# Linear attention, then a gated mixture of causal-attention experts: the work as a task graph, PE's order from a list scheduler

## The chip, the cores and the metric

One core of a Trainium2 chip runs the whole program. The engines are TensorE (PE, with its weight loads as PEld), VectorE (DVE), ScalarE (ACT), GpSimd (POOL) and SyncE (SP, which issues the DMAs here). The time is device microseconds of one execution; several executions are run, and one more is profiled.

## The reference

Eight batches, eight heads of 64, 576 tokens. The first half is linear attention without a softmax, normalised for each head; the second half gives each token its two best of four experts, each of which is a causal attention over the batch's tokens.

```python
kv = einsum('bhsd,bhse->bhde', k, v)
out = einsum('bhsd,bhde->bhse', q, kv)
x = out / sqrt(mean(out * out, -1) + 1e-6) * g_norm      # heads side by side: (8, 576, 512)
logits = x @ w_gate                                      # 4 experts; softmax over the best 2
for e in range(4):
    q, k, v = x @ wq[e], x @ wk[e], x @ wv[e]            # 64 wide
    a = softmax(causal(q @ k.T / 8))
    result += gate[e] * (a @ v @ wo[e])
```

## The kernel before

Each batch goes through three stages. The 576 tokens are five blocks (four of 128, one of 64); heads and experts are taken in pairs. PSUM is cut into three "big" buffers of two banks and two "small" ones of one bank, and every product on PE takes one of them.

Stage A (stage_a): p_kv is k by v for each head, over the tokens; it is copied to kvx (DVE) and, padded to two heads side by side, to kv2 (ACT). kv2 is transposed on PE (p_kt, L216), copied to kvT, and multiplied by the gate weights (p_kg, L224, four products), so that four more columns per head in kvx give the gate's logits. q is transposed block by block (p_q, L200, copied to qT by DVE). Then p_out (L242) is q by kvx for each block; DVE copies it to the one o_sb (L249), ACT squares it out of p_out (L253), DVE sums the squares (L259). A row of small DVE instructions makes the inverse root (L270 to L280) and the logits (L285, L291), and POOL scales o_sb to x_tok (L297).

Stage X (stage_x): x_tok is transposed on PE (p_x, L313) and copied by ACT to xT.

Stage S (stage_s): DVE makes the gate; p_v (L355), then for each pair of experts the projections p_proj (L373), copied by ACT to qTp and kT (L384, one copy for both experts, 64 partitions each). The scores p_sc (L400) contract over the 64 partitions of one expert; five pieces a pair; ACT takes their exp to PT (L410), POOL masks the diagonal blocks (L415). p_O (L451) is PT by v with a column of ones; DVE divides and gates it (L467 to L472) to osc, which is transposed (p_OT, L484). The stage final gives p_y (L506), copied by ACT and stored by SP.

The order: every stage is a Python generator that yields after each step the PE time that its writer gives it. merge takes from three streams at a time, by these times: stage S of batch b (whose own steps follow a string of letters), stage X of batch b + 1 and stage A of batch b + 2. This gives the program order; the framework then sets the order of every engine's instructions, PE's too, from that program order and from what it finds ready by its own timing. Loads of batch b + 3 are issued at the start of turn b. The three projection weights are loaded to one staging buffer, one after the other (L158), and scaled by g_norm on DVE (L159).

Of the kernel before, what the change touches and what calls it, by code (L numbers as in the profile page):

```python
# [14 lines left out]
AX_X = mybir.AxisListType.X  # L15


@with_exitstack
def kernel(
# [45 lines left out]
    def small(shape, name, dtype=FP32):
        return ps1.tile(shape, dtype, tag="small", name=name)
# [6 lines left out]
    kr, vr, kvx, kv2s, sqs, lg8s, kTs, vexts, mss = [], [], [], [], [], [], [], [], []  # L73
    for j in range(2):
# [16 lines left out]
        nc.gpsimd.memset(t[:], 1.0)  # L91
        vexts.append(t)
        t = const.tile([P, NB, H], FP32, name=f"ms{j}")
        nc.gpsimd.memset(t[REM:P, NF], 1.0)
        mss.append(t)
    ob = const.tile([P, NB, H, GW], FP32, name="o_sb")
    nc.gpsimd.memset(ob[REM:P, NF], 0.0)
    for j in range(3):
        t = const.tile([P, H, Dh + 1], FP32, name=f"sq{j}")
        nc.gpsimd.memset(t[:, :, Dh : Dh + 1], 1e-6)  # L100
        sqs.append(t)
    zpad = const.tile([P, NB * P - S], FP32, name="zpad")
    nc.gpsimd.memset(zpad[:], 0.0)
    for j in range(3):
        t = const.tile([P, NB * P], FP32R, name=f"kT{j}")
        nc.vector.tensor_copy(out=t[:, S : NB * P], in_=zpad[:])
        kTs.append(t)


    def load_qkv(b, fine=False):  # L110
        qt = qkvp.tile([P, NB, H, Dh], FP32, tag="q_b", name="q_b")
        kt = qkvp.tile([P, H, NF, Dh], FP32, tag="k_b", name="k_b")
        vt = qkvp.tile([P, H, NF, Dh], FP32, tag="v_b", name="v_b")

        def main(dst, src, h0, h1):
            nc.sync.dma_start(
                dst[:, h0:h1, :, :].rearrange("p h j d -> p h (j d)"),
                src[b, h0:h1, 0 : NF * P, :].rearrange("h (p j) d -> p h (j d)", j=NF),
            )

        def rem(dst, src):
            nc.sync.dma_start(
                dst[0:REM, :, :], src[b, :, NF * P : S, :].rearrange("h p d -> p h d")
            )

        step = 2 if fine else H
# [12 lines left out]
    loads = {0: load_qkv(0, fine=True)}

    g_wide = const.tile([P, 1], FP32, name="g_wide")
    for r in range(P // Dh):
        nc.sync.dma_start(g_wide[r * Dh : (r + 1) * Dh, :], g_norm.unsqueeze(1))
    wg_st = const.tile([P, NCH, E], FP32, name="wg_st")
    nc.sync.dma_start(wg_st[:], moe_w_gate.rearrange("(c p) e -> p c e", p=P))
    wg_bd = const.tile([P, NCH, 2, E], FP32, name="wg_bd")
    nc.gpsimd.memset(wg_bd[:], 0.0)
    for hh in range(2):
        pp = slice(hh * Dh, (hh + 1) * Dh)
        nc.vector.tensor_scalar_mul(  # L150
            out=wg_bd[pp, :, hh, :], in0=wg_st[pp], scalar1=g_wide[pp]
        )
    w_r = {}
    for name, wdram in (("v", moe_wv), ("q", moe_wq), ("k", moe_wk)):
        wr = const.tile([P, NCH, E, Hd], FP32R, name=f"w{name}_r")
        wf = wst.tile([P, NCH, E, Hd], FP32, name="w_stage", tag="w_stage")
        for e in range(E):
            nc.sync.dma_start(wf[:, :, e, :], wdram[e].rearrange("(c p) f -> p c f", p=P))  # L158
        nc.vector.tensor_scalar_mul(  # L159
            out=wr[:].rearrange("p c e f -> p (c e f)"),  # L160
            in0=wf[:].rearrange("p c e f -> p (c e f)"),
            scalar1=g_wide[:],
        )
        w_r[name] = wr
    loads[1] = load_qkv(1)
    wo_st = wst.tile([P, EP, D], FP32, name="wo_st", tag="w_stage")
    for pr in range(EP):
        nc.sync.dma_start(
            wo_st[:, pr, :], moe_wo[2 * pr : 2 * pr + 2].rearrange("two d m -> (two d) m")
        )  # L170
    wo_b = const.tile([P, EP, D], BF16, name="wo_b")
    nc.vector.tensor_copy(out=wo_b[:], in_=wo_st[:])

    def kv_pair(p_kv, c, kb, vb, krem, vrem):
        for j in range(NF + 1):
            for hh in range(2):
                h = 2 * c + hh
                lk, rv = (kb[:, h, j, :], vb[:, h, j, :]) if j < NF else (krem[:, h, :], vrem[:, h, :])
                nc.tensor.matmul(  # L179
                    p_kv[hh * Dh : (hh + 1) * Dh, c, :], lhsT=lk, rhs=rv,  # L180
                    start=(j == 0), stop=(j == NF), skip_group_check=True,
                )

    def kv_copy(p_kv, kvb, kv2):
        for hh in range(2):
            pp = slice(hh * Dh, (hh + 1) * Dh)
            nc.vector.tensor_copy(out=kvb[pp, :, hh, 0:Dh], in_=p_kv[pp, :, :])
            nc.scalar.copy(kv2[pp, :, hh * Dh : (hh + 1) * Dh], p_kv[pp, :, :])  # L188


    def stage_a(b, res):
        qb, kb, vb = loads[b]
        qT = s1.tile([P, NCH, S], FP32, tag="qT", name="qT", bufs=1)
        kvb, kv2 = kvx[b % 2], kv2s[b % 2]

        def q_block(i):
            t0, nt = blocks[i]
            p_q = small([P, NCH, P], "p_q")
            for c in range(NCH):
# [341 lines left out]
    for _ in y_gen:  # L541
        pass
# [30 lines left out]
```

## Time and profile before

| | us |
|---|---|
| median of three runs | 328.1 (328.66, 324.1, 328.1) |
| the profiled execution | 324.47 |
| its span, first to last instruction | 322.5 |
| PE busy (share of the span) | 276.0 (86%) |
| PEld, weight loads | 220.4 (68%) |
| DVE | 189.2 (59%) |
| ACT | 153.0 (47%) |
| POOL | 79.5 (25%) |
| mean granted clock of TensorE | 0.945 |

An engine's busy time is the time in which at least one of its instructions runs; the end of a matmul is modelled, so that neighbours overlap in it. A clock of 1.00 is 2.4 GHz, 0.50 is 1.2 GHz.

### The profile page before, as it was taken

The numbers are of one execution on the slowest core, as the hardware profiler recorded it, in microseconds if no ns is written. First come the engines' busy times: TensorE is split into PE (matmuls) and PEld (weight loads), VectorE is DVE, ScalarE is ACT, GpSimd is POOL, SyncE is SP. The second block draws the span as 40 slices with busy tenths as digits, with TensorE's granted clock in tenths as the row PEclk, the third lists the DMA queues.
The fourth block names the chain that finished last, engine by engine and source line by source line (L and its number), as shares of the span: only waits on it lengthen the run. The fifth ranks groups of instructions, "written<-read, shape, count | busy, mean of one in ns | idle before, by whom it ended". The sixth has DMA issues, their size and how long they took to land.

```text
span 322.5 us, 6704 instructions
## 1 busy us (share of the span) xinstructions
PE 276.0 (86%) x2624; PEld 220.4 (68%) x2624; DVE 189.2 (59%) x537; ACT 153.0 (47%) x273; POOL 79.5 (25%) x148
## 2 busy tenths in 40 slices
PE   1675579799979997999889996999889996999984
PEld 1565468588858775887667875887667875867641
DVE  0249948846884568646775578546774578424130
ACT  0203123653464654545554554545555554585843
POOL 8100600441044110702053101612052101630210
PEclk9959599999999999799999999799999999899977
DMA  6977999999704269194608372001200120021124
GB/s 195 243 199 195 205 301 223 298 180 276 152 2 133 64 202 192 41 253 127 169 3 269 81 182 58 2 0 67 82 2 2 65 83 0 0 100 53 65 83 147
DMA packets 75280, 40.30 MB, mean 125 GB/s; under 512 B 54000, under 2 KB 70384, under 8 KB 75248
## 3 DMA queue, kind: packets, MB, share of 16 engines
q1 hardware_dynamic: 75248, 39.86, 47.1%
q8 instruction: 21, 0.34, 0.5%
q14 instruction: 11, 0.09, 0.1%
HBM read 30.42 MB, written 9.44 MB: 124 GB/s over the span
## 4 chain that ended last, share of the span: by engine, by line
PE 70%; DVE 10%; ACT 9%; SPq 4%; issue 3%; POOL 1%; DMA 1%; DVEq 0%; ACTq 0%; POOLq 0%
PE p_proj L373 11%; PE p_out L242 11%; PE p_v L355 7%; PE p_sc L400 7%; PE p_O L451 7%; PE p_y L506 6%; PE p_q L200 6%; PE p_x L313 6%; PE p_kv L179 5%; ACT PT L410 3%; PE p_kg L224 3%; DVE o_sb L249 3%; SPq L134 2%; PE p_OT L484 2%; POOL x_tok L297 1%
## 5 line engine op out<-in xcount | busy, mean ns | idle before, releaser
L415 POOL TENSOR_SCALAR_AFFINE_SELECT PT<-PT 128x256 bf16<-128x256 bf16 (+1 forms) x80 | 29.3, 381 | 143.4 <-ACT PT L410 143.4
L410 ACT ACTIVATE PT<-p_sc 128x576 bf16<-128x576 f32 (+3 forms) x80 | 53.9, 714 | 20.1 <-PE p_sc L400 18.1
L297 POOL TENSOR_TENSOR x_tok<-o_sb,y 128x512 f32<-128x512 f32 (+1 forms) x40 | 42.0, 1080 | 85.1 <-DVE y L280 85.0
L242 PE MATMUL p_out<-kvx,qT 128*128 128x136 f32 (+1 forms) x320 | 48.1, 292 | 0.0
L400 PE MATMUL p_sc<-qTp,kT 64*128 64x288 f32 (+2 forms) x192 | 35.7, 358 | 10.7 <-ACT PT L410 5.9
L242 PEld LDWEIGHTS p_out<-kvx,qT 128*128 128x128 f32 (+1 forms) x320 | 40.2, 181 | 4.8 <-ACT sq L253 2.1
L253 ACT ACTIVATE sq<-p_out 128x512 f32<-128x512 f32 (+1 forms) x40 | 23.8, 596 | 39.9 <-DVE o_sb L249 38.4
L318 ACT CAST xT<-p_x 128x512 fp32r<-128x512 f32 (+1 forms) x40 | 21.8, 545 | 34.3 <-PE p_x L313 34.3
L400 PEld LDWEIGHTS p_sc<-qTp,kT 64*128 64x128 f32 x192 | 19.8, 185 | 21.9 <-ACT PT L410 8.5
L179 PE MATMUL p_kv<-v_b,k_b 128*64 128x64 f32 x512 | 25.7, 260 | 10.3 <-DMA v_b<-in_v_dram 10.3
L249 DVE COPY o_sb<-p_out 128x544 f32<-128x544 f32 (+1 forms) x40 | 28.7, 719 | 7.7 <-PE p_out L242 7.2
L362 DVE CAST vext<-p_v 128x256 bf16<-128x256 f32 (+1 forms) x40 | 17.0, 425 | 26.3 <-PE p_v L355 25.6
L259 DVE TENSOR_REDUCE ms<-sq 128x8 f32<-128x520 f32 (+1 forms) x40 | 27.4, 688 | 7.9 <-ACT sq L253 7.8
L205 DVE COPY qT<-p_q 128x512 f32<-128x512 f32 (+1 forms) x40 | 24.7, 634 | 11.6 <-PE p_q L200 11.0
L451 PEld LDWEIGHTS <-PT 128*128 128x128 bf16 (+2 forms) x480 | 24.1, 103 | 10.8 <-issue 5.3
L179 PEld LDWEIGHTS p_kv<-v_b,k_b 128*64 128x64 f32 x512 | 23.0, 173 | 12.2 <-DMA k_b<-in_k_dram 6.7
L451 PE MATMUL p_O<-vext,PT 128*128 128x65 bf16 (+2 forms) x480 | 30.3, 199 | 0.4 <-ACT PT L410 0.4
L313 PE MATMUL p_x<-ident_f,x_tok 128*128 128x128 f32 (+1 forms) x160 | 25.9, 289 | 5.4 <-POOL x_tok L297 4.3
L355 PE MATMUL p_v<-wv_r,xT 128*128 128x256 f32 (+1 forms) x160 | 28.3, 300 | 0.7 <-ACT kv L188 0.7
L373 PE MATMUL p_proj<-xT,wk_r 128*128 128x288 f32 x128 | 24.3, 314 | 3.6 <-ACT qTp L384 3.6
L506 PE MATMUL p_y<-wo_b,OT 128*128 128x512 bf16 (+1 forms) x80 | 25.1, 417 | 0.7 <-ACT OT L489 0.7
L511 ACT COPY y<-p_y 128x512 f32<-128x512 f32 (+1 forms) x40 | 23.0, 595 | 5.0 <-PE p_y L506 2.7
(67 smaller groups left out, 360.9 us busy)
## 6 DMA issues: line engine op xcount, KB each, us to landing
q_b<-in_q_dram SPq DMA_DIRECT2D x32, 256.0 KB, 5.2
out_dram<-y SPq DMA_DIRECT2D x32, 256.0 KB, 2.1
k_b<-in_k_dram SPq DMA_DIRECT2D x7, 1024.0 KB, 6.0
v_b<-in_v_dram SPq DMA_DIRECT2D x7, 1024.0 KB, 10.2
k_b<-in_k_dram SPq DMA_DIRECT2D x4, 256.0 KB, 4.7
v_b<-in_v_dram SPq DMA_DIRECT2D x4, 256.0 KB, 4.9
k_rem<-in_k_dram SPq DMA_DIRECT2D x8, 128.0 KB, 9.2
v_rem<-in_v_dram SPq DMA_DIRECT2D x8, 128.0 KB, 7.5
```

The costliest lines, as they stand in the source:

```text
L179: nc.tensor.matmul(p_kv[hh * Dh : (hh + 1) * Dh, c, :], lhsT=lk, rhs=rv, start=(j == 0), stop=(j == NF), skip_group_check=True,)
L242: nc.tensor.matmul(p_o[:nt, c // 2, (c % 2) * 2 * GW : (c % 2 + 1) * 2 * GW], lhsT=qT[:, c, t0 : t0 + nt], rhs=kvb[:, c, :, :].rearrange(" ...
L249: nc.vector.tensor_copy(out=ob[:nt, i].rearrange("p (k h) g -> p k (h g)", k=2), in_=p_o[:nt, :, 0 : 4 * GW])
L297: nc.gpsimd.tensor_tensor(out=xt[:nt], in0=ob[:nt, i, :, 0:Dh], in1=y[:nt, i * H : (i + 1) * H].unsqueeze(2).to_broadcast([nt, H, Dh]), op ...
L313: nc.tensor.transpose(p_x[:, c, :nt], xts[i][:nt, 2 * c : 2 * c + 2, :].rearrange("p h d -> p (h d)"), ident_f[:nt, :nt],)
L355: nc.tensor.matmul(p_v[:nt, :], lhsT=xT[:, c, t0 : t0 + nt], rhs=w_r["v"][:, c, :, :].rearrange("p e f -> p (e f)"), start=(c == 0), stop= ...
L373: nc.tensor.matmul(p_p[:, s, 0:HALF], lhsT=w_r[nm][:, c, 2 * pr : 2 * pr + 2, :].rearrange("p e f -> p (e f)"), rhs=xT[:, c, s * HALF : (s ...
L400: nc.tensor.matmul(p_s[:, el, o : o + hi - lo], lhsT=kTp[pb, kb * P : (kb + 1) * P], rhs=qTp[pb, lo:hi], start=True, stop=True,)
L410: nc.scalar.activation(PT[:, :, d0 : d0 + o], p_s[:, :, 0:o], ACTF.Exp, scale=scale)
L415: nc.gpsimd.affine_select(out=d, in_=d, compare_op=AluOpType.is_ge, fill=0.0, base=0, pattern=[[0, 2], [1, w]], channel_multiplier=-1,)
L451: nc.tensor.matmul(p_O[:nq, bank, (2 * n + el) * (Hd + 1) : (2 * n + el + 1) * (Hd + 1)], lhsT=PT[:nk, el, col : col + nq], rhs=vx[:nk, kb ...
L506: nc.tensor.matmul(p_y[:nq, :], lhsT=OT[:, pr, s0 : s0 + nq], rhs=wo_b[:, pr, :], start=(pr == 0), stop=(pr == EP - 1),)
```

## The change

The program is written again as tasks. graph names each task with its engine, a time for which it holds the engine, a time to its result, the tasks that it needs and the buffers that it uses. plan goes through them as a list scheduler: at each step it takes the task that can start first on any engine, and among those of that engine that can start within 0.02 of it the one with the least urgency value; a buffer is taken with the first task that uses it and given back after the last. Urgency is the batch's number times PERIOD plus an offset for each kind of task, with steps within a kind. The tasks are written out in the order of their planned start. Under manual_schedule PE keeps just that order. The instructions of DVE, ACT, POOL and SP are written in the same order too, but the framework orders them as it did before.

Some of the work changes its form. k and v of batches after the first are loaded in two pieces. The projection weights are loaded in halves to six buffers, which are those of x_tok. The p_kv copy of ACT is one copy without padding, p_kt has two transposes of two head pairs packed together in place of four, p_kg two products in place of four, and its copy to kvx is two. ACT's square reads o_sb. kT is now four buffers, one for each of the four experts, with the 64 partitions of the other expert of the pair zero; ACT copies each half by itself, and the scores contract over 128 partitions. The other tasks do what the functions of before do. The middle of the diff, with the parts that are only moved left out:

```diff
+def graph(B):
+    t = {}
+
+    def add(name, eng, hold, lat, needs=(), tiles=()):
+        t[name] = (eng, hold, lat, [n for n in needs if n in t], list(tiles))
+
+    def pe(name, hold, needs, tiles=()):
+        add(name, "PE", hold, hold + 0.27, needs, tiles)
...
+    R5, R4, R2 = range(NB), range(NCH), range(EP)
+    for b in range(B):
+        for p in R4 if b == 0 else R2:
+            w = 1.0 if b == 0 else 2.0
+            tl = (("k", b), ("v", b))
+            add(("lk", b, p), "SP", 0.5, 0.45 * w, [("kv", b - 2, c) for c in R4] if p == 0 else [], tl[:1])
+            add(("lv", b, p), "SP", 0.5, 0.45 * w, [("kv", b - 2, c) for c in R4] if p == 0 else [], tl[1:])
...
+            for nm in "qkv":
+                for p in R2:
+                    add(("lw", nm, p), "SP", 1.0, 1.3, (), (("x", nm, p),))
+                    dve(("ws", nm, p), 0.48, [("lw", nm, p), ("lg0",)], (("x", nm, p),))
...
+        for c in R4:
+            piece = c if b == 0 else c // 2
+            pe(("kv", b, c), 0.88, [("lk", b, piece), ("lv", b, piece), ("lr", b)], (("sm", "kv", b), ("k", b), ("v", b)))
+        dve(("kvx", b), 0.84, [("kv", b, c) for c in R4] + [("out", b - 2, i) for i in R5], (("sm", "kv", b),))
+        act(("kvc", b), 0.37, [("kvx", b), ("kt", b - 2)], (("sm", "kv", b),))
...
+        pe(("kt", b), 0.22, [("kvc", b)], (("sm", "kt", b),))
+        dve(("ktc", b), 0.42, [("kt", b)], (("sm", "kt", b), ("kvT", b)))
+        pe(("kg", b), 0.45, [("ktc", b), ("wg",)], (("sm", "kg", b), ("kvT", b)))
+        dve(("kgc", b), 0.34, [("kg", b)] + [("out", b - 2, i) for i in R5], (("sm", "kg", b),))
+        for i in R5:
+            pe(("out", b, i), 0.93, [("qc", b, i), ("kvx", b), ("kgc", b)], (("bg", "out", b, i), ("qT", b)))
+            dve(
+                ("oc", b, i), 0.73, [("out", b, i), ("xm", b - 1, i), ("gl", b - 1), ("sq", b - 1, i)],
+                (("bg", "out", b, i),),
+            )
+            n = NB * b + i - 3
+            act(("sq", b, i), 0.60, [("oc", b, i), ("red", n // NB, n % NB)])
+            dve(("red", b, i), 0.69, [("sq", b, i), ("nw", b - 2, 10)])
...
+        for p in R2:
+            for nm in "qk":
+                pe((nm + "p", b, p), 1.06, xT + [("ws", nm, 0), ("ws", nm, 1)], (("bg", nm, b, p), ("xT", b)))
+            act(("qpc", b, p), 0.64, [("qp", b, p)], (("bg", "q", b, p), ("qTp", b, p)))
+            act(("kpc", b, p), 1.24, [("kp", b, p)] + [("sc", b - 1, p, j) for j in R5], (("bg", "k", b, p),))
+            hold = (0.25, 0.25, 0.39, 0.28, 0.29)
+            took = (0.66, 0.66, 0.95, 0.72, 0.60)
+            for j in R5:
+                pe(("sc", b, p, j), hold[j], [("qpc", b, p), ("kpc", b, p)], (("bg", "sc", b, p, j), ("qTp", b, p)))
+                act(("exp", b, p, j), took[j], [("sc", b, p, j)], (("bg", "sc", b, p, j), ("PT", b, p)))
+                if j != 1:
+                    pool(("msk", b, p, j), 0.41 if j < 4 else 0.70, [("exp", b, p, j)])
...
+        for i in R5:
+            pe(("y", b, i), 0.45, [("otc", b, 0), ("otc", b, 1), ("wo", "o", 0), ("wo", "o", 1)], (("sm", "y", b, i), ("OT", b)))
+            act(("yc", b, i), 0.59, [("y", b, i)], (("sm", "y", b, i), ("y", b, i)))
+            add(("st", b, i), "SP", 0.1, 0.9, [("yc", b, i)], (("y", b, i),))
+    return t
+
+
+NF = 4
+POOLS = {
+    "k": 2, "v": 2, "q": 2, "sm": 2, "bg": 3, "qT": 1, "kvT": 2, "gl": 2, "x": 6, "xT": 2, "gate": 2,
+    "qTp": 3, "PT": 3, "osc": 2, "inv": 2, "OT": 2, "y": 4,
+}
+PERIOD = 25.7
+OFFSET = dict(
+    lk=-101.2, lv=-101.2, lr=-101.2, lq=-86.0, lg0=-200, wg=-60, lw=-35.8, ws=-10.8, lwo=-85, wo=-30,
+    kv=-61.6, kvx=-60.6, kvc=-60.6, q=-57.9, qc=-75.4, kt=-138.5, ktc=-138.5, kg=-137.5, kgc=-137.5,
+    out=-27.6, oc=112.9, sq=29.9, red=-136.3, nw=93.2, gl=94.2, lg=95.2, xm=24.8, x=-29.3, xc=-80.7,
+    m8=19.2, sh=19.2, ex=19.2, mk=19.2, gt=19.2, den=19.2, rd=19.2, gate=19.2, v=2.0, vc=-91.6, qp=40.7,
+    qpc=12.5, kp=35.4, kpc=7.2, sc=-1.2, exp=-49.5, msk=4.3, pv=-109.0, rc=-99.4, iv=-99.4, oc2=-99.4,
+    ot=13.9, otc=13.9, y=26.5, yc=-17.4, st=26.5,
+)
+STEP = dict(
+    x=1.5, xc=2.0, out=1.9, oc=1.9, sq=1.9, red=1.9, v=0.9, vc=0.5, y=1.7, yc=2.0, st=1.6, lq=1.5,
+)
+SECOND = 9.2
+
+def urgency(n):
+    kind = n[0]
+    if len(n) == 1 or isinstance(n[1], str):
+        return OFFSET[kind] + ("qkvo".index(n[1]) if len(n) > 1 else 0.0)
+    o = n[1] * PERIOD + OFFSET[kind]
+    if kind in STEP:
+        o += n[2] * STEP[kind]
+    elif kind in ("qp", "qpc", "kp", "kpc", "sc", "exp", "msk", "pv", "rc", "iv", "oc2", "ot", "otc"):
+        o += n[2] * SECOND + (0.4 * n[3] if len(n) > 3 else 0.0)
+    elif kind == "kv":
+        o += 0.1 * n[2]
+    return o
+
+def plan(tasks, pools, prio):
+    slots = {p: [0.0] * n for p, n in pools.items()}
+    users, need, waits = {}, {}, {}
+    for n, (_, _, _, needs, tiles) in tasks.items():
+        for tl in tiles:
+            users[tl] = users.get(tl, 0) + 1
+        need[n] = len(needs)
+        for m in needs:
+            waits.setdefault(m, []).append(n)
+    cand = {e: set() for e in ("PE", "ACT", "DVE", "POOL", "SP")}
+    for n in tasks:
+        if not need[n]:
+            cand[tasks[n][0]].add(n)
+    free = {e: 0.0 for e in cand}
+    ready, held, last, dma, order, end = {n: 0.0 for n in tasks}, set(), {}, 0.0, [], 0.0
+    none = 1e9
+    while len(order) < len(tasks):
+        starts = []
+        for eng, ns in cand.items():
+            f = free[eng]
+            for n in ns:
+                t = ready[n]
+                for tl in tasks[n][4]:
+                    if tl not in held:
+                        t = max(t, min(slots[tl[0]], default=none))
+                if eng == "PE" and t > f - 0.15:
+                    t += 0.1
+                starts.append((max(t, f), prio[n], eng, n))
+        t0, _, eng, _ = min(starts)
+        t, _, _, n = min(((t, p, e, n) for t, p, e, n in starts if e == eng and t <= t0 + 0.02), key=lambda x: x[1])
+        assert t < none
+        _, hold, lat, _, tiles = tasks[n]
+        cand[eng].discard(n)
+        for tl in tiles:
+            if tl not in held:
+                held.add(tl)
+                slots[tl[0]].remove(min(slots[tl[0]]))
+        free[eng] = t + hold
+        fin = t + lat
+        if eng == "SP":
+            dma = max(dma, t + hold + 1.3) + lat
+            fin = dma + 0.5
+        end = max(end, fin)
+        order.append((t, len(order), n))
+        for tl in tiles:
+            users[tl] -= 1
+            last[tl] = max(last.get(tl, 0.0), fin)
+            if not users[tl]:
+                slots[tl[0]].append(last[tl])
+        for m in waits.get(n, ()):
+            need[m] -= 1
+            ready[m] = max(ready[m], fin)
+            if not need[m]:
+                cand[tasks[m][0]].add(m)
+    order.sort()
+    return order, end
...
+    kTs = []
+    for pr in range(EP):
+        pair = []
+        for el in range(2):
+            t = const.tile([P, NB, P], FP32R, name=f"kT{pr}{el}")
+            other = slice((1 - el) * Hd, (2 - el) * Hd)
+            nc.vector.tensor_copy(
+                out=t[other], in_=zrow[other].unsqueeze(1).to_broadcast([Hd, NB, P])
+            )
+            nc.vector.tensor_copy(out=t[:, NF, REM:P], in_=zrow[:, REM:P])
+            pair.append(t[:].rearrange("p n t -> p (n t)"))
+        kTs.append(pair)
...
+    def lw(nm, m):
+        wf = buf(("x", nm, m), [P, 2, E, Hd], FP32, "w_stage")
+        for c in range(2):
+            rows = slice((2 * m + c) * P, (2 * m + c + 1) * P)
+            nc.sync.dma_start(wf[:, c, :, :], w_dram[nm][:, rows, :].rearrange("e p f -> p e f"))
...
+    def kvc_copy(b):
+        nc.scalar.copy(kvcs[b % 2][:], small(None, "kv", b)[:])
...
+    def kt(b):
+        p_kt = small([P, EP, P], "kt", b)
+        for m in range(EP):
+            nc.tensor.transpose(
+                p_kt[:, m, :], kvcs[b % 2][:, 2 * m : 2 * m + 2, :].rearrange("p c e -> p (c e)"), ident_f[:]
+            )
...
+    def kg(b):
+        p_kg = small([P, EP, 2, 2, E], "kg", b)
+        for m in range(EP):
+            nc.tensor.matmul(
+                p_kg[:, m].rearrange("p c a e -> p (c a e)"),
+                lhsT=tiles["kvT", b][:, m, :],
+                rhs=wg_bd[:, m].rearrange("p c a e -> p (c a e)"),
+                start=True,
+                stop=True,
+            )
...
+    def sq_act(b, i):
+        nt = blocks[i][1]
+        nc.scalar.activation(
+            sqs[(NB * b + i) % 3][:nt, :, 0:Dh], ob[:nt, i, :, 0:Dh], ACTF.Square, scale=1.0 / (Dh**0.5)
+        )
...
+    def k_proj_copy(b, pr):
+        for el in range(2):
+            pb = slice(el * Hd, (el + 1) * Hd)
+            nc.scalar.copy(
+                kTs[pr][el][pb, 0:S].rearrange("p (s n) -> p s n", s=2), big("k", b, pr)[pb, :, 0:HALF]
+            )
...
+    def sc(b, pr, j):
+        p_s = big("sc", b, pr, j)
+        o = 0
+        for kb, lo, hi in PIECES[j]:
+            for el in range(2):
+                nc.tensor.matmul(
+                    p_s[:, el, o : o + hi - lo],
+                    lhsT=kTs[pr][el][:, kb * P : (kb + 1) * P],
+                    rhs=tiles["qTp", b, pr][:, lo:hi],
                     start=True,
                     stop=True,
                 )
...
+    tasks = graph(B)
+    with tc.manual_schedule(engines={mybir.EngineType.PE}):
+        for _, _, n in plan(tasks, POOLS, {n: urgency(n) for n in tasks})[0]:
+            emit[n[0]](*n[1:])
```

## Rows read from the trace of the kernel before

**Rows 1.** The page, part 1: busy us, share and instructions of each engine.
```profile
PE 276.0 (86%) x2624; PEld 220.4 (68%) x2624; DVE 189.2 (59%) x537; ACT 153.0 (47%) x273; POOL 79.5 (25%) x148
```
**Rows 2.** Windows by stage: busy us of each engine, granted clock, DMA share, GB/s.
```profile
0.00:20.00 20.00, 8.48 (x96) 7.21 (x97) 3.50 (x10) 2.02 (x3) 8.42 (x28) 0.94 0.86 206
20.00:40.00 20.00, 13.11 (x97) 11.39 (x99) 16.53 (x41) 4.29 (x8) 5.01 (x5) 0.67 0.84 209
...
180.00:216.00 36.00, 33.37 (x325) 27.31 (x325) 22.40 (x66) 18.66 (x34) 8.79 (x15) 0.95 0.25 67
...
273.00:322.00 49.00, 41.95 (x320) 28.06 (x320) 15.14 (x59) 29.89 (x52) 12.40 (x25) 0.89 0.21 74
```
**Rows 3.** The chain that ended last, in order of time: start, us, what.
```profile
55.54 1.26 PE p_proj L373 x8
...
63.55 2.48 PE p_kv L179 x80
...
107.64 0.99 PE p_kg L224 x8
...
202.94 3.62 PE p_kv L179 x80
...
252.31 0.99 PE p_kg L224 x8
```
**Rows 4.** PE's timeline in one steady turn: start, us, what, count.
```profile
183.55 1.04 PE L200 MATMUL p_q<-ident_f,q_b 128*128 128x128 f32 x8
184.42 0.41 PE L451 MATMUL p_O<-vext,PT 128*128 128x65 bf16 x8
...
187.77 1.19 PE L242 MATMUL p_out<-kvx,qT 128*128 128x136 f32 x8
188.80 0.52 PE L484 MATMUL p_OT<-ident_b,osc 128*128 128x128 bf16 x5
189.25 0.60 PE L506 MATMUL p_y<-wo_b,OT 128*128 128x512 bf16 x2
189.69 1.09 PE L242 MATMUL p_out<-kvx,qT 128*128 128x136 f32 x8
...
199.94 0.62 PE L400 MATMUL p_sc<-qTp,kT 64*128 64x288 f32 x4
...
209.04 0.74 PE L355 MATMUL p_v<-wv_r,xT 128*128 128x256 f32 x4
209.62 0.60 PE L313 MATMUL p_x<-ident_f,x_tok 128*128 128x128 f32 x4
210.15 0.35 PE L400 MATMUL p_sc<-qTp,kT 64*128 64x192 f32 x1
...
214.53 0.91 PE L373 MATMUL p_proj<-xT,wk_r 128*128 128x288 f32 x5
215.28 0.60 PE L216 MATMUL p_kt<-ident_f,kv 128*128 128x128 f32 x4
215.72 0.60 PE L200 MATMUL p_q<-ident_f,q_b 128*128 128x128 f32 x4
```
**Rows 5.** Waits of three turns, 144 to 252 us: total, times, longest.
```profile
ACT sq L253 <- DVE o_sb L249: 11.1, 6, 2.6
...
PEld p_sc L400 <- ACT PT L410: 3.5, 3, 1.2
...
PEld p_sc L400 <- ACT kT L384: 3.0, 7, 0.8
```
**Rows 6.** Windows of 2 us around one p_kv: columns as in rows 2.
```profile
200.00:202.00 2.00, 1.07 (x10) 0.54 (x8) 1.79 (x11) 1.83 (x4) 1.34 (x2) 1.00 0.00 0
202.00:204.00 2.00, 2.00 (x26) 1.67 (x27) 0.96 (x2) 1.74 (x3) 2.00 (x3) 0.50 0.00 0
```
**Rows 7.** Groups by line over the whole span: busy us, mean ns, idle before.
```profile
L384 ACT CAST kT<-p_proj 128x576 fp32r<-128x576 f32 x16 | 10.2, 639 | 18.7 <-PE p_proj L373 18.7
```
**Rows 8.** DVE's timeline at the start.
```profile
38.45 1.30 DVE L159 TENSOR_SCALAR wk_r<-w_stage,g_wide 128x1024 fp32r<-128x1024 f32 x1
```

More of the change, by code (lines that the diff above doesn't have):

```diff
@@ L162, with lwo @@
             scalar1=g_wide[:],
         )
[L164 to L174, printed above, removed]
+    def lwo(_, pr):
+        t = buf(("y", "wo", pr), [P, D], FP32, "wo_st")
+        nc.sync.dma_start(t[:], moe_wo[2 * pr : 2 * pr + 2].rearrange("two d m -> (two d) m"))
@@ L175, in kv_pair, with wo, kv @@
+    def wo(_, pr):
+        nc.vector.tensor_copy(out=wo_b[:, pr, :], in_=tiles["y", "wo", pr][:])
+    def kv(b, c):
+        p_kv = small([P, NCH, Dh], "kv", b)
         for j in range(NF + 1):
@@ new lines, in xm, with x_tr, x_copy @@
+    def xm(b, i):
+        nt = blocks[i][1]
+        nc.gpsimd.tensor_tensor(
+            out=buf(("x", b, i), [P, H, Dh], FP32, "x_tok")[:nt],
+            in0=ob[:nt, i, :, 0:Dh],
+            in1=st["rstd", b][:nt, i * H : (i + 1) * H].unsqueeze(2).to_broadcast([nt, H, Dh]),
+            op=AluOpType.mult,
+        )
+    def x_tr(b, i):
+        transpose_in(i, tiles["x", b, i], "x", b, i)
+    def x_copy(b, i):
+        t0, nt = blocks[i]
+        xT = buf(("xT", b), [P, NCH, S], FP32R, "xT")
+        nc.scalar.copy(xT[:, :, t0 : t0 + nt], small(None, "x", b, i)[:, :, :nt])
@@ new lines, in rd, with gate, v_mm @@
+    def rd(b):
+        nc.vector.reciprocal(small_t(b, "rd", [P, NB]), st["den", b][:])
+    def gate(b):
+        nc.vector.tensor_tensor(
+            out=buf(("gate", b), [P, NB, E], FP32, "gate")[:], in0=st["gt", b][:],
+            in1=st["rd", b][:].unsqueeze(2).to_broadcast([P, NB, E]), op=AluOpType.mult,
+        )
+    def v_mm(b, i):
+        t0, nt = blocks[i]
+        p_v = small([P, E * Hd], "v", b, i)
+        for c in range(NCH):
+            nc.tensor.matmul(
+                p_v[:nt, :],
+                lhsT=tiles["xT", b][:, c, t0 : t0 + nt],
+                rhs=w_r["v"][:, c, :, :].rearrange("p e f -> p (e f)"),
+                start=(c == 0),
+                stop=(c == NCH - 1),
+            )
@@ new lines, in v_copy, with proj @@
+    def v_copy(b, i):
+        nt = blocks[i][1]
+        nc.vector.tensor_copy(
+            out=vexts[b % 2][:nt, i, :, 0:Hd], in_=small(None, "v", b, i)[:nt].rearrange("p (e f) -> p e f", e=E)
+        )
+    def proj(nm, b, pr):
+        p_p = big(nm, b, pr)
+        for c in range(NCH):
+            for s in range(2):
+                nc.tensor.matmul(
+                    p_p[:, s, 0:HALF],
+                    lhsT=w_r[nm][:, c, 2 * pr : 2 * pr + 2, :].rearrange("p e f -> p (e f)"),
+                    rhs=tiles["xT", b][:, c, s * HALF : (s + 1) * HALF],
+                    start=(c == 0),
+                    stop=(c == NCH - 1),
+                )
@@ L502, in final @@
-    def final(b, OT):
-        for qc, (s0, nq) in enumerate(blocks):
-            p_y = small([P, D], "p_y")
-            for pr in range(EP):
-                nc.tensor.matmul(
-                    p_y[:nq, :], lhsT=OT[:, pr, s0 : s0 + nq], rhs=wo_b[:, pr, :],
-                    start=(pr == 0), stop=(pr == EP - 1),
-                )
-            y = ysb.tile([P, D], FP32, tag="y", name="y")
-            nc.scalar.copy(y[:nq, :], p_y[:nq, :])
-            nc.sync.dma_start(out[b, s0 : s0 + nq, :], y[:nq, :])
-            yield 0.45
@@ new lines, in ot_copy, with y_mm, y_copy @@
+    def ot_copy(b, pr):
+        nc.scalar.copy(buf(("OT", b), [P, EP, S], BF16, "OT")[:, pr, :], small(None, "ot", b, pr)[:])
+    def y_mm(b, qc):
+        s0, nq = blocks[qc]
+        p_y = small([P, D], "y", b, qc)
+        for pr in range(EP):
+            nc.tensor.matmul(
+                p_y[:nq, :], lhsT=tiles["OT", b][:, pr, s0 : s0 + nq], rhs=wo_b[:, pr, :],
+                start=(pr == 0), stop=(pr == EP - 1),
+            )
+    def y_copy(b, qc):
+        nq = blocks[qc][1]
+        nc.scalar.copy(buf(("y", b, qc), [P, D], FP32, "y")[:nq, :], small(None, "y", b, qc)[:nq, :])
```

698 lines of the change are left out of this document (314 added, 384 removed).

## Prediction

> **What bounds the kernel now.** First the page's busy shares: PE has work for 86% of the span, DVE 59%, ACT 47% [rows 1]. Then the table by stage: in a steady turn PE is busy 33.4 of 36 us, with only the first 40 us (21.6 busy) and the last 49 us (42 busy) thinner [rows 2]. So PE is the engine to look at, but "busy" joins instructions whose modelled ends overlap, and hides waits of up to some 0.2 us. The chain of waits gives the true period: the gate product p_kg of one batch to that of the next, four turns between the first and the last row, (252.31 - 107.64) / 4 = 36.2 us [rows 3]. The question is how much of 36.2 is work that any order must do.
>
> For that I read start-to-start times in the timeline of one steady turn, where the next group starts with no idle time before it [rows 4]. Per batch, at full clock: p_kv 2.48 [rows 3]; p_q 0.87 for two blocks, so 2.1 for four and a half; p_kt 0.44; p_kg 0.99 [rows 3]; p_out 1.03 a block, 5.15; p_x 0.53 a block, 2.5; p_v 0.58 a block, 2.9; p_proj 0.15 a matmul, 32 of them, 4.8; p_sc 0.31 a pair of heads (four matmuls in 0.62), 12 pairs, 3.7; p_OT 0.45 twice, 0.9; p_y 0.44 a block, 2.2. p_O has 60 small matmuls: the row gives 0.051 each (0.41 by 8) with the drain of the last inside it, so I take 0.04, 2.4 in all, with 3.0 as the upper bound. The sum is 30.6 us. The other 5.6 us of a turn are waits and switches: PE waiting for ACT's exp of the scores or its copy of kT [rows 5], and a score or a p_v put alone between others, since the framework interleaves PE instruction by instruction (a single p_x block, then one half of a score pair, then p_v [rows 4]). One more cost stands in the clock: after PE was busy 1.07 of 2 us (200 to 202) the granted clock is 0.50 in the next two, so 1.2 GHz [rows 6], and p_kv takes 3.62 instead of 2.48 us [rows 3].
>
> **The change, part by part.** *The order.* PE now runs a list written ahead, with whole tasks kept together: 51 tasks a batch (kv 4, q 5, kt, kg, out 5, x 5, v 5, projections 4, scores 10, pv 4, ot 2, y 5), chosen with the other engines' times in the plan, across three batches. It adds no PE work. What it can win is the 5.6 us and the slow p_kv. I take it that 1.0 us of the waits stays in each turn: the two named waits on p_sc in rows 5 make (3.5 + 3.0) / 3 = 2.2 us a turn, and a plan that puts another batch's work there keeps about half. Bounds: 0, and all 5.6.
>
> *Gate product.* p_kt and p_kg work on pairs of heads packed two to a transpose: half the matmuls, so 0.44 + 0.99 becomes about 0.72. Minus 0.7 a batch on PE. ACT's two half copies become one; DVE's copy of p_kg becomes two small ones. Both engines have over 40% idle, nothing on the path.
>
> *Scores.* Each head's kT gets its own buffer with the other head's 64 rows zero, so a score contracts over 128 rows, not 64. A full-row matmul of 288 columns takes 0.15 (p_proj), two make 0.30, against 0.31 for a pair now [rows 4]: nothing. The bound: were the pair now one matmul's time, 0.15, the change would cost 0.15 x 12 = 1.8 us a batch. The Trainium skill ("TensorEngine Tiling (Array Packing)", section Tiling Modes) says that tiles of different rows of the array can load and multiply in parallel, up to twice as fast for a contraction of 64, but that a change of tiling mode drains the array. By the first half this edit gives away a factor of two on the scores; the pair's 0.31 shows nothing of that factor, and the second half speaks for the edit.
>
> *ACT.* The copy of kT becomes two, of half the partitions but the same free size: 16 more of 0.64 us [rows 7], +10.2 us in all, 1.3 a batch. ACT goes from 153 to about 160 of some 285, 56%, under PE's share. But a copy of kT stands directly before the scores, and now two stand there: 0.64 later each time, 16 times; hidden as long as the order puts another batch's p_out, p_v, p_y, p_x or p_q in between (15 us of those a batch), 10 us if not. I count it inside the 1.0.
>
> *Square from o_sb.* ACT's square reads o_sb in SBUF rather than p_out; it already comes after DVE's copy to o_sb, for which it waits 11.1 us in three turns [rows 5], so nothing is later, and the PSUM buffer comes free about 0.6 us earlier. Zero, or a small gain within the 5.6.
>
> *Loads.* By the offsets batch 0 loads first, then wo, batch 1's k, v and q, then batch 2's k and v if p_kv of batch 0 has freed their buffers, and only then the projection weights. By shapes: 3.54 + 0.52 + 3.54 + 1.57 = 9.2 MB, with batch 2's k and v 11.5. The first two stages moved 206 and 209 GB/s, 8.3 MB by 40 us [rows 2]; so the last weights land between 44 and 55. Now the last weight is scaled at 38.45 [rows 8] and the first projection stands at 55.5 [rows 3], after batch 1's p_out. The weights also stage in the six x buffers, so x of batch 0 waits for them, and p_out of batch 1, whose o_sb is single, waits for that x. Until then PE has some 16 us of work (all of batch 0 up to p_out, batch 1 up to p_kg), where before 23 were done by 55. Projections then start between 46 and 56: in the early case PE is 9 us ahead with 7 us less done, in the late one level with 7 less done, and it has idled more at the lower clock before. That is -3 to +12 on the idle time of the start; I take +6. Later k and v loads come in two pieces and stand with the stores in SP's queue in the plan's order; the DMA share of a steady turn is 0.25 [rows 2], so a load has several turns to land: nothing. The fills at the start (POOL without kv2 and most of vext, DVE with the zero halves of kT) lie before the first loads have landed: nothing.
>
> **How the numbers follow.** PE work per batch 30.6 - 0.7 = 29.9, eight batches 239. Idle in the first 40 us 18.4 [rows 2], plus 6. The lower clock of the first 40 us (0.67 over the 13.1 busy us of the second stage) 4. Waits 1.0 in seven turns, 7. The end, 7 idle of 49 [rows 2] and its clock of 0.89 on 42, 5 more. Sum 239 + 18.4 + 6 + 4 + 7 + 7 + 5 = 286 us of span, against 322.5. The profiled execution took 324.5, 2 more than its span, and lies 1% under the median of the runs, 328.1, among runs from 324 to 329. So 288 us, read against 328: an eighth less. The same from before's side: 36.2 - 30.9 = 5.3 less a turn, eight turns, 42, less the 6 of the start. From 2% on (321.5 and 334.7) a change of this kernel can be told from none.
>
> **The rivals.** *Dense* (0.17): the plan leaves PE almost no waits, the clock stays at 2.4 GHz and p_O costs 0.03 each: minus 7, minus some 5 of clock, minus 5, and no loss at the start, minus 6: 265. For it speaks that the timeline of before has long stretches with no gap, p_out and p_y alternating for 5 us [rows 4]; against it that the other engines are not in the plan's order.
>
> *The waits stay* (0.18): PE's list is fixed, the others run as the framework finds them ready by its own clock, and PE, which can't take another task meanwhile, loses half of what it won: 2.3 us a turn back, 306. At the full 5.6 only the smaller gate product is left: about 317. For it: every wait on p_sc in rows 5 is for ACT, which gets more to do just there.
>
> *Row tiles mattered* (0.04): scores cost the full 1.8 more a batch: 288 + 14 = 302. By the skill's factor it would be so; the pair's 0.31 is against it.
>
> *Slower* (0.08): head-of-line blocking. In a fixed list each of 408 tasks waits for its operand even when another could run. If the order of DVE or ACT differs so that a task waits 0.10 us longer on average than I count, all is lost (40 / 408); at 0.15 it is 349. Against it: DVE and ACT would still have over a third of the time free (189 and 160 of 286), and the deepest wait named for PE is 1.2 us once a turn [rows 5].
>
> The forecast, 276 to 300, has 0.53. Two in ten may be left out: the upper end takes in the waits that stay and the row tiles, 317; the lower end is the dense case, 266. Faster by over 2%: 0.53 + 0.17 + 0.04 and nearly all of the waits that stay, 0.12 of 0.18, 0.86; within 2%, the worst of those waits, 0.06; slower 0.08.
>
> **What would show it.** Right: the page shows PE at 90% or more of a shorter span; p_kg of successive batches 31 us apart; PE's waits on p_sc for ACT a third of before's; p_kv at 2.5 us in every turn; p_sc at full rows 0.30 a pair; ACT near 160 us busy; the first projection between 46 and 56 us. Wrong: PE idle at p_x or p_out for DVE or POOL (the framework's order), p_sc groups longer than 0.35 a pair (row tiles), the first projection later than 58 (loads), or a granted clock under 0.9 in the steady part, which would mean that PE still halts long enough for it to fall.

## The result

The changed kernel takes 305.1 us (median of four runs, 304.5 to 305.2) against 326.1 for the one before on the same chip: ratio 0.938, interval 0.929 to 0.947. The forecast was 288, with 266 to 317 around it: the direction is right, the gain is a little over half of the forecast. The profiled execution's span is 303.4 us where the sum gave 286.

Page of the changed kernel, part 1, against [rows 1]:

```profile
PE 257.0 (85%) x2576; PEld 222.5 (73%) x2576; DVE 187.1 (62%) x554; ACT 159.1 (52%) x281; POOL 77.0 (25%) x146
```

Its windows by stage, in us, columns as in [rows 2]:

```profile
0.00:20.00 20.00, 5.85 (x87) 5.19 (x88) 5.68 (x13) 1.66 (x2) 5.66 (x26) 0.97 0.74 188
20.00:40.00 20.00, 13.29 (x145) 12.21 (x143) 16.18 (x45) 3.37 (x6) 2.17 (x2) 0.84 1.07 235
40.00:66.00 26.00, 19.11 (x184) 17.38 (x185) 15.97 (x29) 7.55 (x14) 3.34 (x3) 0.83 1.04 249
66.00:108.00 42.00, 37.99 (x348) 33.54 (x346) 32.71 (x100) 17.18 (x31) 13.99 (x20) 0.87 0.83 198
108.00:139.00 31.00, 29.69 (x307) 25.46 (x307) 17.95 (x64) 22.46 (x41) 9.64 (x18) 1.00 0.35 94
139.00:169.00 30.00, 26.34 (x259) 22.90 (x259) 21.94 (x61) 15.72 (x30) 7.88 (x13) 0.94 0.38 105
169.00:200.00 31.00, 29.88 (x296) 26.34 (x296) 21.34 (x63) 21.88 (x39) 9.38 (x16) 1.00 0.66 157
200.00:231.00 31.00, 29.71 (x326) 26.05 (x328) 22.13 (x71) 20.04 (x36) 8.95 (x15) 1.00 0.12 41
231.00:262.00 31.00, 30.04 (x327) 26.55 (x327) 22.40 (x70) 20.25 (x36) 8.95 (x15) 1.00 0.11 40
262.00:303.00 41.00, 35.14 (x315) 26.91 (x313) 10.77 (x47) 28.96 (x51) 7.05 (x19) 0.99 0.25 88
```

Its chain that ended last, against [rows 3] (p_q at L633 is a projection; p_q at L433, further down, is the transposed q):

```profile
65.34 1.92 PE p_q L633 x8
...
200.00 2.48 PE p_kv L415 x80
...
230.93 2.48 PE p_kv L415 x80
```

The steady turn is what was forecast: 230.93 - 200.00 = 30.9 us against 36.2, p_kv at 2.48 both times (3.62 at 202.94 in [rows 3]), the clock at 1.00, PE busy 29.7 to 30.0 a turn. What was lost lies before 169 us: PE idle for 28 us up to 66, for 4.0 in the next 42 with the clock at 0.87, and for 3.7 in the 30 from 139.

How the start goes: SP's timeline, then the waits of the stretch 40 to 66.

```profile
35.65 0.62 SPq L352 DMA_DIRECT2D k_b<-in_k_dram  x1
...
39.39 5.92 SPq L392 DMA_DIRECT2D w_stage<-in_moe_wq_dram  x4
45.35 2.73 SPq L392 DMA_DIRECT2D w_stage<-in_moe_wk_dram  x4
48.18 4.74 SPq L369 DMA_DIRECT2D q_b<-in_q_dram  x5
...
54.24 1.10 SPq L392 DMA_DIRECT2D w_stage<-in_moe_wv_dram  x2
...
59.42 1.68 SPq L392 DMA_DIRECT2D w_stage<-in_moe_wv_dram  x2
```

```profile
PE p_q L433 <- DVE qT L443: 5.7, 1, 5.7
PE p_kt L448 <- ACT kvc L427: 5.6, 1, 5.6
DVE wv_r L395 <- DMA w_stage<-in_moe_wv_dram: 5.0, 1, 5.0
```

The weights are issued from 39 us on, the last at 59, behind k and v of batch 2, q of batch 2 and a part of batch 3's k and v. DVE stands 5.0 us in its queue for a piece of wv; the copy of p_q is behind it, and PE, held to its list, waits 5.7 for that copy. The stall of the stretch from 139 is of another kind, in the timeline:

```profile
157.48 4.04 POOL L553 TENSOR_TENSOR x_tok<-o_sb,rs 128x512 f32<-128x512 f32 x4
...
157.99 2.57 DVE L588 TENSOR_TENSOR mk<-lg,m 128x20 f32<-128x20 f32 x1
160.48 1.08 DVE L579 TENSOR_TENSOR sh<-lg,m 128x20 f32<-128x20 f32 x1
161.48 0.74 DVE L625 CAST vext<-p_v 128x256 bf16<-128x256 f32 x2
...
161.94 0.70 PE L747 MATMUL p_y<-wo_b,OT 128*128 128x512 bf16 x2 [3.60 <-DVE vext L625]
```

Two gate instructions of 20 columns take 2.57 and 1.08 us beside POOL's x_tok, the p_v copy stands behind them, and PE is idle for 3.6. So the three longest waits of PE behind its first load, 5.6, 5.7 and 3.6 us, are all for something that stands behind other work in DVE's queue.

### The profile page after: what moved, and what is told of

Its sections match the earlier page's. It is cut to its first block, busy times and chain, and to the rows that moved or that the text cites. A ratio compares the mean times of both kernels' runs of the same rounds, so it can differ in the third digit from the quotient of the medians.

```text
span 303.4 us, 6611 instructions
## 1 busy us (share of the span) xinstructions
PE 257.0 (85%) x2576; PEld 222.5 (73%) x2576; DVE 187.1 (62%) x554; ACT 159.1 (52%) x281; POOL 77.0 (25%) x146
## 4 chain that ended last, share of the span: by engine, by line
PE 52%; DVE 19%; SPq 9%; DMA 8%; ACT 6%; issue 2%; POOL 2%; ACTq 0%; DVEq 0%; POOLq 0%
PE p_out L478 9%; PE p_sc L659 8%; PE p_x L433 5%; PE p_q L433 5%; PE p_pv L695 5%; PE p_kv L415 5%; SPq L352 4%; PE p_v L615 3%; PE p_q L633 3%; PE p_y L747 3%; PE p_k L633 3%; DMA v_rem<-in_v_dram 3%; DMA w_stage<-in_moe_wv_dram 2%; DVE inv L719 2%; DMA w_stage<-in_moe_wq_dram 2%
## 5 line engine op out<-in xcount | busy, mean ns | idle before, releaser
L553 POOL TENSOR_TENSOR x_tok<-o_sb,rs 128x512 f32<-128x512 f32 (+1 forms) x40 | 41.8, 1068 | 89.6 <-DVE rs L529 65.8
L679 POOL TENSOR_SCALAR_AFFINE_SELECT PT<-PT 128x256 bf16<-128x256 bf16 (+1 forms) x80 | 29.9, 384 | 123.8 <-ACT PT L673 123.2
L494 ACT ACTIVATE sq<-o_sb 128x512 f32<-128x512 f32 (+1 forms) x40 | 25.3, 635 | 36.6 <-DVE o_sb L488 36.5
L659 PE MATMUL p_sc<-qTp,kT 128*128 128x288 f32 (+2 forms) x192 | 37.9, 322 | 3.9 <-DVE inv L715 1.9
L659 PEld LDWEIGHTS p_sc<-qTp,kT 128*128 128x128 f32 x192 | 28.4, 192 | 10.5 <-issue 3.5
L415 PE MATMUL p_kv<-v_b,k_b 128*64 128x64 f32 x512 | 22.9, 237 | 12.1 <-DMA v_b<-in_v_dram 12.1
L433 PE MATMUL p_q<-ident_f,q_b 128*128 128x128 f32 (+1 forms) x160 | 26.9, 301 | 6.1 <-DVE qT L443 5.7
L415 PEld LDWEIGHTS p_kv<-v_b,k_b 128*64 128x64 f32 x512 | 19.9, 149 | 14.1 <-DMA k_b<-in_k_dram 11.5
L695 PE MATMUL p_pv<-vext,PT 128*128 128x65 bf16 (+2 forms) x480 | 26.5, 202 | 0.7 <-DVE osc L726 0.3
L433 PEld LDWEIGHTS p_q<-ident_f,q_b 128*128 128x128 f32 (+1 forms) x160 | 20.1, 160 | 8.8 <-DVE qT L443 6.2
L648 ACT CAST kT<-p_k 64x576 fp32r<-64x576 f32 x32 | 20.3, 634 | 11.9 <-PE p_k L633 11.5
```

Source lines behind the costliest of these rows:

```text
L415: nc.tensor.matmul(p_kv[hh * Dh : (hh + 1) * Dh, c, :], lhsT=lhs, rhs=rhs, start=(j == 0), stop=(j == NF), skip_group_check=True,)
L433: nc.tensor.transpose(p_t[:, c, :nt], src[:nt, 2 * c : 2 * c + 2, :].rearrange("p h d -> p (h d)"), ident_f[:nt, :nt])
L553: nc.gpsimd.tensor_tensor(out=buf(("x", b, i), [P, H, Dh], FP32, "x_tok")[:nt], in0=ob[:nt, i, :, 0:Dh], in1=st["rstd", b][:nt, i * H : (i ...
L659: nc.tensor.matmul(p_s[:, el, o : o + hi - lo], lhsT=kTs[pr][el][:, kb * P : (kb + 1) * P], rhs=tiles["qTp", b, pr][:, lo:hi], start=True, ...
L679: nc.gpsimd.affine_select(out=d, in_=d, compare_op=AluOpType.is_ge, fill=0.0, base=0, pattern=[[0, 2], [1, w]], channel_multiplier=-1,)
L695: nc.tensor.matmul(p_O[:nq, bank, (2 * n + el) * (Hd + 1) : (2 * n + el + 1) * (Hd + 1)], lhsT=PT[:nk, el, col : col + nq], rhs=vexts[b % ...
```

## The experiments

One thing had to be settled first. In plan, tasks of equal urgency are taken in the order in which Python goes through a set of names, which differs from process to process. So builds of the kernel can have different lists; the one measured is one draw. All runs of the changed kernel below settle ties by name; "the control" has besides that PE's list as the trace of the changed kernel shows it. Ratios are to the kernel before, on the same chip; the runs lie on two chips, so between runs the ratios are what counts. The edits are shown in part, with names shortened.

**Control, and two other lists.**

```diff
-        t, _, _, n = min(((t, p, e, n) for ... ), key=lambda x: x[1])
+        t, _, _, n = min(((t, p, e, n) for ... ), key=lambda x: (x[1], repr(x[3])))
-            for n in ns:
+            for n in ns if eng != "PE" else ns & set(todo[:1]):
```

> The changed kernel with PE's list written out as the trace of it shows it, and ties in the planner settled by name, so that each build gives the same order (as it stands, ties between equal urgencies fall as Python happens to order a set, and the list differs from build to build). Control for the others. If PE's list and the framework make the time, it is that of the changed kernel, 305, within 3 us; if the order in which the other engines' tasks are written out matters too, it may differ by 5 or more.

297.5 us, 0.920 (0.915 to 0.925): PE's order in the trace is that of the changed kernel, the time 7.5 less. The written order of the other engines' tasks alone makes that. The trace shows where: the control has the wait of 5.6 for p_kt too, but neither the 5.7 behind wv nor the 3.6 behind the gate; its longest wait of PE after 60 us is 2.1.

> The changed kernel with the planner's ties settled by name, so another list than the one measured. Theory start (the 17 us over the forecast are lost before the first projections, since the weights load behind batches 1 and 2): 300 to 310, since every list has the same order of loads. Theory draw (the measured list was an unlucky one): 285 to 295.

299.7, 0.928 (0.921 to 0.935).

> As the run before, ties settled by the names read backwards: a third list. Theory start: 300 to 310 again. Theory draw: the three lists spread by over 10 us.

294.8, 0.911 (0.905 to 0.917). Three lists with ties by name spread over 5 us, and the measured draw lies 5 above the worst of them. Neither theory's numbers came for it: the third list lies under the 300 of the first and the three do not spread by 10. The draw is worth some 8. The first projection is at 61 to 64 us in these three and at 57.0 in the slower measured draw, so its time does not tell how long the kernel takes.

**Weights first.**

```diff
+        early = [n for n in seq if n[0] == "lw"]
+        seq = [n for n in seq if n[0] not in ("lw",)]
+        at = 1 + max(i for i, n in enumerate(seq) if n[:2] == ("lq", 0))
+        for n in seq[:at] + early + seq[at:]:
```

> The control with the six loads of projection weights issued right after batch 0's q, before batch 1's loads; PE's list unchanged. Theory start: weights scaled by 35 in place of 69, first projection about 10 us earlier, time 290 to 296. Theory framework (the other engines' order costs PE waits in every turn, the start is no worse than forecast): 302 or more.

292.8, 0.905 (0.893 to 0.917): the median is 5 under the control's, within the range expected, but the intervals overlap and the four runs spread from 289.7 to 296.5. The weights are scaled by 38 us, yet the first projection comes only at 57.7, not 10 earlier than the control's 62.5, since PE's list puts batch 1's p_out and batch 2's p_kv before it. The trace is of the fastest run; PE's waits for p_kt fall in it from 7.8 to 4.0 us, but PE now waits 5.0 for v of batch 1, which loads later. That the loads explain a part of the 17 us is not shown.

**All engines held; none held.**

```diff
-    with tc.manual_schedule(engines={PE}):
+    with tc.manual_schedule(engines={PE, DVE, Activation, Pool, SP}):
```

> The control (PE's written list, ties by name) with DVE, ACT, POOL and SP too held to the planned order. Theory start: from 100 us on PE is already busy 30 of 31 us, so nothing is won there; where the plan's order has DVE wait for weights that the plan thinks landed at 45 and that land near 58, it loses: 297 to 305. Theory framework: the other engines' own order is what costs PE its waits: 290 or less.

287.6, 0.882 (0.875 to 0.889), the time of the forecast: the theory of the framework's order, against mine; but most of what is won is won at the start. The loads are as late as in the control: the last weights are scaled at 58 us in both. The waits of PE from 20 to 100 us, first the control, then all held:

```profile
PE p_kt L484 <- ACT kvc L463: 7.8, 2, 5.6
```

```profile
PE p_kt L484 <- ACT kvc L463: 4.1, 2, 2.1
```

In the timeline of the control DVE runs batch 0's inverse root, gl, lg and most of the gate, from 35.3 on, before it copies batch 1's p_kv, for which p_kt waits:

```profile
40.25 0.82 DVE L460 COPY kvx<-p_kv 64x256 f32<-64x256 f32 x2
...
41.58 0.69 PE L484 MATMUL p_kt<-ident_f,kvc 128*128 128x128 f32 x2 [5.64 <-ACT kvc L463]
```

With all held it takes that copy after six of the eleven steps of the root:

```profile
36.26 0.20 DVE L558 SCALAR_TENSOR_TENSOR ru<-rs 128x40 f32<-128x40 f32 x1
36.38 0.85 DVE L460 COPY kvx<-p_kv 64x256 f32<-64x256 f32 x2
...
37.74 0.44 PE L484 MATMUL p_kt<-ident_f,kvc 128*128 128x128 f32 x2 [1.94 <-ACT kvc L463]
```

> The control's tasks, forms and written order, with PE too left to the framework. If holding PE's order is what makes the turn 31 us: the turn goes back towards 34 to 36, time 310 to 325. If the written order and whole tasks do it and holding adds nothing: within 3 us of the control, 298.

292.7, 0.898 (0.890 to 0.906): neither expectation. With the same written order, PE free is 2% faster than PE held alone, and the turn is still 31 us in its trace. Holding PE is not what makes the turn; holding it while the others run as the framework likes costs 2% here, most of it before 100 us. That cost is not more waiting: PE is busy 71.5 of the first 100 us in both traces, at a granted clock of 0.93 with none held and 0.88 in the control. Over the four runs of each, the mean clock is 0.965 to 0.976 against 0.947 to 0.954. The wait for p_kt is 5.7 us with none held too, so it comes of DVE's order and not of the held list.

**The list made for the loads as they land, then with all held.**

```diff
-            add(("lk", b, p), "SP", 0.5, 0.45 * w, ...
+            add(("lk", b, p), "SP", 0.5, 1.1 * w, ...
-    lw=-35.8
+    lw=-84.0
```

> The changed kernel with ties by name, the planner told 1.1 us for 256 KB of k or v (233 GB/s, what the trace shows) in place of 0.45, and the projection weights urgent right behind batch 0: a list made for the loads as they land. Theory start: better than the weights moved alone (293), since PE's list no longer waits for batch 1 ahead of batch 0's projections: 284 to 290, first projection at 45 to 52. If the start is bound by the bytes alone: 293 to 298.

290.4, 0.891 (0.883 to 0.899), between the two. The last weights are scaled by 34, but the plan fills in other work in front of batch 0's projections, which still start at 60.6, not at 45 to 52.

> The list made for the loads as they land, with all engines held to it. If the two gains add (4% for holding all, 3% for the loads): 279. If both repair the same start: 285 to 290.

287.2, 0.879 (0.872 to 0.887), the time of all held without it: the gains do not add. These two are the best versions found. They are not the same repair, though, as the traces side by side show (one execution each; PE's busy time and granted clock are those of the windows 0 to 100 and 100 to 259 us):

| | us | first projection | PE busy, 0 to 100 | clock there | PE busy, 100 to 259 |
|---|---|---|---|---|---|
| changed kernel | 305.1 | 57.0 | 70.1 | 0.86 | 149.8 |
| control | 297.5 | 62.5 | 71.5 | 0.88 | 153.4 |
| weights first | 292.8 | 57.7 | 72.1 | 0.95 | 153.9 |
| none held | 292.7 | 61.1 | 71.5 | 0.93 | 154.1 |
| all held | 287.6 | 58.7 | 76.9 | 0.91 | 154.8 |
| list for the loads | 290.4 | 60.6 | 69.8 | 0.93 | 155.4 |
| list for the loads, all held | 287.2 | 60.7 | 71.5 | 0.90 | 157.9 |

Holding all engines wins PE's time at the start. The list for the loads wins none there; it wins in the turns, which are 29.8 us long in it with all held (p_kv at 148.6 and, two turns on, at 208.1). The time of the first projection does not order these kernels: the fastest two have it at 58.7 and 60.7, the slowest at 57.0.

**Scores over 64 rows again.**

```diff
-                    lhsT=kTs[pr][el][:, kb * P : (kb + 1) * P],
-                    rhs=tiles["qTp", b, pr][:, lo:hi],
+                    lhsT=kTs[pr][el][el * Hd : (el + 1) * Hd, kb * P : (kb + 1) * P],
+                    rhs=tiles["qTp", b, pr][el * Hd : (el + 1) * Hd, lo:hi],
```

> The control with the scores over the 64 rows of one expert again (copies of kT as in the control, in halves). Theory full rows cost nothing: a pair 0.30 against 0.31, time within 3 us of 298. Theory row tiles (two halves run at once): the pair falls to about 0.15, 1.8 us a batch less, 284. Theory switch (each change between 64-row and 128-row matmuls drains PE): 10 visits a batch at about 0.1, 306.

294.7, 0.906 (0.897 to 0.915): 1% below the control, the intervals just touch. The windows of p_sc alone over three steady turns, control and then 64 rows (PE, PEld and ACT busy):

```profile
166.00:259.00 93.00, 15.81 (x80) 11.72 (x80) 21.39 (x33) 1.00 0.24 66
```

```profile
166.00:259.00 93.00, 10.43 (x80) 6.53 (x80) 23.19 (x35) 1.00 0.22 62
```

The row tiles do overlap: 80 matmuls busy for 10.4 us in place of 15.8, 1.8 us a turn. The Trainium skill ("TensorEngine Tiling (Array Packing)", section Tiling Modes) says that different tiles can load weights and multiply in parallel; the trace agrees. But the turn gets at most some 0.3 us shorter, and PE's whole busy time in these 93 us falls only from 89.2 to 87.3: where the rest goes, no run took apart.

> The kernel before with the scores alone changed: kT in one buffer an expert with zero halves, two copies on ACT, contraction over 128 rows (the output buffers of y fall from four to three and kT's from three sets to two, for room). Theory nothing: 320 to 330. Theory switch (64-row matmuls put alone between 128-row ones drain PE in this interleaved order): 10 us less or more, 310 to 316. Theory row tiles: 14 us longer, 338.

325.5, 1.004 (0.999 to 1.010): done alone in the kernel before, with its second copy on ACT, the change is worth nothing in the whole. Its trace shows two parts that cancel: p_kg of batch 2 comes at 81.9 us in place of 76.0, and the four turns from batch 3 to batch 7 are 34.9 each in place of 36.2 on average, with the p_kv of the chain at 2.48 there. What of this is the scores' was not taken apart.

**The square out of PSUM again.**

```diff
-            sqs[...][:nt, :, 0:Dh], ob[:nt, i, :, 0:Dh], ACTF.Square, ...
+            sqs[...], big("out", b, i)[...][:, :, :, 0:Dh], ACTF.Square, ...
```

> The control with ACT's square out of p_out again, so that a PSUM buffer is kept 0.6 us longer, five times a batch. If the earlier release counts for nothing: within 3 us of the control, 297. If it is a part of the gain in the turn: 31.0 becomes 32 or more, 303 or later.

296.7, 0.911 (0.900 to 0.921): the control's time. The earlier release counts for nothing.

**The kernel before with PE held to merge's order.**

```diff
+    with tc.manual_schedule(engines={mybir.EngineType.PE}):
         merge((stage_a(0, res[0]), CA, 0.0, 1.0))
...
```

> The kernel before with PE alone held to its program order (the steps of merge, each whole), nothing else changed. Theory interleaving (the framework mixes PE's steps instruction by instruction, and that is most of the 5.6 us a turn): turn 36.2 to about 33, time 300 to 308. Theory head-of-line (holding PE alone costs, as the control lost against the free one): the turn grows, 330 or more.

386.4, 1.183 (1.171 to 1.195): the second theory, and far beyond its 330. Its page, a window of one turn (p_kg to p_kg 44.5 us), and PE's waits:

```profile
PE 302.1 (78%) x2624; PEld 240.6 (62%) x2624; DVE 188.9 (49%) x537; ACT 155.5 (40%) x273; POOL 80.3 (21%) x148
```

```profile
196.00:242.00 46.00, 38.06 (x355) 30.87 (x356) 23.00 (x67) 19.77 (x35) 10.03 (x17) 0.83 0.39 104
```

```profile
PE p_x L313 <- POOL x_tok L297: 23.7, 7, 5.7
PE p_O L451 <- DVE osc L472: 22.7, 15, 2.8
```

PE stands up to 5.7 us at a time for x_tok and 2.8 for osc, where the kernel before, with the same work, has the framework put other steps in between; and the granted clock of the stretch falls to 0.83. The framework's mixing of steps, which I had read as a cost, hides more than it costs. In merge's order the steps are not placed by when the plan has their operands ready; in the graph's they are.

## Why the prediction was half right

- *The order*: 29.9 of work and 1.0 of waits gave 30.9 a turn; 30.9 was measured. The mechanism that I named for it was wrong in one point: I counted the framework's mixing among the losses, and took the held list for the gain. With none held the turn is 31 too, and in the kernel before holding costs 18%. What shortens the turn is the written order together with the forms of the tasks. That is by elimination: holding PE, the square and the full rows were undone one at a time, and none of them makes the turn. How the rest shares out, beyond the 0.7 us of p_kt and p_kg that are counted, no run here took apart; the kernel before's own forms in the graph's order were not run.
- *Waits* is the term that failed. The sum had 1.0 us in each of seven turns, and at the start, beyond 6 for the loads, nothing for PE standing behind the framework's order of the other engines; I priced that only in two rivals. The changed kernel waits 5.6, 5.7 and 3.6 us for work behind others in DVE's queue, all before 169 us; the control, with another order of the other engines' tasks, has only the first. From the control to all held only the order of DVE, ACT, POOL and SP changes, and the time is the forecast's. PE then loses some 30 us of the first 100 (23.1 idle, 76.9 busy at 0.91), which is what the sum had: 18.4 + 6 + 4 and the waits of two turns. The changed kernel loses 40 there. In its own windows PE is idle 27.8 us to 66 in place of 24.4, and 9.0 between 66 and 169 in place of some 3. By busy time times what the granted clock lacks, the lower clock takes 2.1 + 3.2 + 4.9 = 10 us up to 108 and 1.6 from 139 to 169, where 4 were counted for the start. PE's work, busy time times clock, adds up to 245 in place of 239; which part of it was priced too low, no run took apart.
- *Loads*: the first projection is at 57.0 us, the second at 65, and I had 46 to 56 (the weights stand behind more than the 11.5 MB that I reckoned with, since q of batch 2 and a part of batch 3 go before wv too). But that was not the loss. I took PE to have some 16 us of work before the projections; by busy time times clock it does 29.7 up to 56.9, since the list puts batch 1's p_out and batch 2's p_kv there, and the kernel before does 29.2 up to its own first projection. With all held the first projection is later still, at 58.7, and the time is the forecast's. Where late weights show as a wait is DVE: 5.0 us for a piece of wv in this draw, 0.3 in all in the control from 40 to 66.
- *The waits stay* is the rival whose 306 was measured, and its cause, PE fixed among engines in the framework's order, is the right one; but it priced 2.3 us in every turn, and the steady turn has none of that. The waits lie before 169 us, so that the number fits is luck. (Its 317 for the worst case is 5.6 taken from the span; as a time it would be some 322.)
- *One draw*: that the list differs from build to build was not seen in plan, and 7.5 us hang on how the other engines' ties fell (0.938 against 0.920, intervals apart).
- *Scores*: no cost and no gain for the whole, as forecast, but the pair's 0.31 had been read wrongly. The row of four matmuls at 199.94 holds two of 288 and two of 448 columns, though it is labelled by its first, and the trace of the kernel before has the two halves of a pair start together: at 199.689 and 199.695, at 201.414 and 201.417. At full rows, in the control, the second of a pair of 288 columns starts 0.13 to 0.24 later. So the overlap could be read before the change; over all scores it is a third.
- *ACT*: 159.1 us against 160 forecast. *Square*: nothing, as forecast. *End*: 5.9 idle against 7, and the clock at 0.99 rather than 0.89, a gain of some 6 over the forecast. PE is busy 85% of the span, not the 90% that I named as a sign.

## What to carry to other kernels

A list scheduler's order can be dense on the chip in its steady turn and thin at the start. Its times should be those of the trace (it counts 0.45 us for 256 KB of k or v, some 580 GB/s, where the trace shows 235 to 249 GB/s from 20 to 66 us), but putting them right made the turns denser here and not the start. If one engine's order is fixed, try fixing the others' too: PE held alone was 2% slower than none held and 4% slower than all held with one list, and within the noise of all held with another. Held to an order that was not planned for it, it was 18% slower. Compare versions by PE's busy time and granted clock in the same windows, not by when one step starts. Make ties in a planner deterministic before timing it, or several builds are needed to know what was timed.

## What the runs showed of the hardware

In the changed kernel a DVE TENSOR_TENSOR on 128 by 20 elements took 0.16 to 0.18 us when POOL ran no x_tok product. Beside such products, of some 1.04 us each, the same kinds took between 0.17 and 1.3 us, and once 2.57, which ended with the third of four products in a row. In the kernel before, one of them (sh) took 0.95 to 0.96 beside x_tok in all eight batches, and the next (mk) 0.17. Two score matmuls of 64 rows started together overlap: 10.4 us busy against 15.8 for the same 80 at full rows. In the kernel before with PE held, PE was idle 7.9 of 46 us, in waits of up to 5.7, and its granted clock was 0.83 over that stretch.
